# Fused attention and feed-forward layer: the first loads of v and of the weights wait for VectorE's first scores

## The chip, the cores and the metric

The kernel runs on one core of a Trainium2 chip. The metric is the device time of one execution in microseconds (us). Three runs of the kernel before took 865.44, 869.37 and 870.81 us; the median is 869.37 us.

The engines are called as in the profile: PE is TensorE (matmuls; PEld its weight loads), DVE is VectorE, ACT is ScalarE, POOL is GpSimd, SP is SyncE, which here only issues DMAs. SPq and ACTq are DMA issues on those two engines' queues.

## The reference

Sparse attention over 8 batches, 8 heads, 576 positions and a head size of 64, then a gated feed-forward layer over all 4608 tokens (512 to 2048 to 512), all in float32:

```python
scores = scale * np.matmul(q, k.transpose(0, 1, 3, 2))
mask_local = (rel >= 0) & (rel < stride)                    # stride = 32, heads 0 to 3
mask_strided = (rel >= 0) & (pos[None, :] % stride == pos[:, None] % stride)   # heads 4 to 7
scores = np.where(masks[None, :, :, :], scores, -1000000000.0)
attn = softmax(scores)          # exp of scores minus the row's maximum, divided by the sum plus 1e-9
x = np.matmul(attn, v)          # heads side by side: (4608, 512)
h = x @ w_in
g = h * np.clip(h + 3.0, 0.0, 6.0) / 6.0
out = g @ w_out
```

(`softmax` stands for three lines of the reference.)

## The kernel before, in words

**Attention.** A unit of work is a pair of heads of one batch (`pair`, L441). Batch 0 is pairs 0 to 3 in the order 0, 2, 1, 3 of their columns: in the names of tiles the digit is that column, so `qn_0`, `v_00` and `v_01` belong to the first pair (local heads), `v_2` to the second (strided heads), `v_10` and `v_11` to the third (local) and `v_3` to the fourth (strided). For the pairs of batch 0 the chain is this:

- q and k are loaded in rows (L492); PE turns them upright with an identity matrix into PSUM (`qp`, `kp`, L372), and DVE or ACT copies them to SBUF (L516, L514).
- PE forms the scores block by block (`ps`, L609 for local heads, L601 for strided ones). DVE adds the mask to the local ones (L634) and sets a corner of 32x32 (L636); ACT copies the strided ones (L627).
- Maximum and sum over rows are DVE's (L645, L659, L662), the subtraction and the scaling POOL's (L649, L666), exp is ACT's (L653).
- The first pairs of local heads are turned again by PE (`pe`, L372), copied by ACT (L723) and multiplied with windows of v (`pv`, L389); the strided ones are transposed by DVE (L685) and multiplied at L738. ACT and DVE write the result as a high and a low half (L427, L430): these are x.

v of a local pair of batch 0 is loaded by six DMAs (`load_half_windows`, L374): overlapping windows of 64 positions, each row of a head a piece of 64 floats, 256 bytes. A strided pair takes four DMAs (L567). Both are issued by SP in `load_v`.

**Feed-forward.** Three tiles of 512 tokens are computed directly (`ffn`, L821): `ph` is x times w_in (L859 to L861, three matmuls, since each float32 factor is a high and a low half), ACT and DVE form the gate (L779, L782), ACT and POOL split it (L793, L797), `acc` is its product with w_out (L836 to L838). The rest goes through a scheme of fast matrix products with fewer multiplications; the change does not touch it.

**Weights.** w_in and w_out are cut into 32 parts of 128 x 512 (`weight_part`, L261; k is the part's number, four parts of w_in, four of w_out and so on). A part is loaded by one DMA of 512 KB on SP (L274, `rawi` or `rawo`), and then made into two halves by ACT (L282, L286), DVE (L290) and POOL or ACT (L304, L306, L309).

**The order.** No engine's order is written by hand. Every step is given to a planner (`Plan`, L61) by `op(engine, us, fn, reads, writes, due, ...)`: an engine, an assumed duration, the keys that it reads and writes, a due time, and for loads `early`, the time before which it isn't issued, and `after`, the time that the transfer is assumed to take. `emit` (L91) plays this through: the engine that can start first takes the step that can start first, of equal ones the one with the earlier due time. From this come the order of instructions on each engine and the places at which PE gets filler matmuls (`idle`, L1564): wherever PE would be without work for 0.64 us or more in the first 100 us of the plan, a 128x384 matmul on the identity matrix is put in (L1573), which the profile shows as "PE idle". The order is fixed when the program is built; on the chip each instruction waits for what it depends on, and what stands behind it on its engine waits with it.

At the start, SP issues two loads of q and ACT two of k, SP two more of q and two of k, and then the first v, as soon as VectorE has cleared its edges.

Of the kernel before, what the change touches and what calls it, by code (L numbers as in the profile page):

```python
# [28 lines left out]
PAD = 32  # L29
# [31 lines left out]
class Plan:  # L61
# [12 lines left out]
    def op(self, engine, us, fn, reads=(), writes=(), due=0.0, room=0.0, mode="", after=0.0, take=None, give=None, early=0.0):  # L74
        n = len(self.ops)
        before = set()
        for k in reads:
            if k in self.wrote:
                before.add(self.wrote[k])
            self.used.setdefault(k, []).append(n)  # L80
        for k in writes:
            if k in self.wrote:
                before.add(self.wrote[k])
            before.update(self.used.pop(k, ()))
            self.wrote[k] = n
        before.discard(n)
        how = engine if isinstance(engine, dict) else {engine: us}
        self.ops.append((how, fn, before, due, room, mode, after, take, give, early))
        return n
# [85 lines left out]
def attention_ffn(ctx: ExitStack, tc, q, k, v, w_in, w_out, out):  # L175
    nc = tc.nc
# [21 lines left out]
    op = plan.op  # L198
    tiles = {}
# [61 lines left out]
    def weight_part(k, w, g, i):  # L261
        key = wkey(w, g, i)
        fc = FQ * g if w == "i" else FQ * g + i + 1
        due = T0 + fc * TILE / NFC - 5.0 + 0.01 * k
        fkey = ("x", 1, 1 - (k // 2 % 2 if k < 20 else 0), k % 2)
        name = f"{w}{g}{i}"

        def load():
            if w == "i":
                src = w_in[i * P:(i + 1) * P, g * TOK:(g + 1) * TOK]  # L270
            else:
                src = w_out[(g * FQ + i) * P:(g * FQ + i + 1) * P, :]
            raw = new(wp, key, [P, TOK, 2], I32, f"raw{name}")
            nc.sync.dma_start(raw, src.bitcast(I32).rearrange("p (n t) -> p n t", t=2))  # L274

        def bits():
            raw = tiles[key]
            return raw.rearrange("p n t -> p (n t)")[:, :TOK]

        def high():  # L280
            f = new(xp, fkey, [P, TOK], I32, f"f{name}")
            nc.scalar.activation(f.bitcast(F32), tiles[key][:, :, 1].bitcast(F32), AF.Prelu, scale=2.0 ** -112, alpha=2.0 ** 32)  # L282

        def low():
            raw = tiles[key].bitcast(U16).rearrange("p n (t u) -> p n t u", u=2)[:, :, 0, 1]
            nc.scalar.activation(bits(), raw, AF.Copy, scale=2.0 ** -13, bias=2.0 ** -14 - 0.5)  # L286

        def join():
            f = tiles[fkey]
            nc.vector.scalar_tensor_tensor(out=f, in0=f, scalar=3, in1=bits(),  # L290
                                           op0=ALU.logical_shift_left, op1=ALU.bitwise_or)

        def whole():
            f = tiles[fkey].bitcast(F32)
            return f if w == "i" else f.rearrange("p (h e d) -> p h d e", h=2, d=2)

        def part(x):
            t = tiles[key][:, x]
            return t if w == "i" else t.rearrange("p (h d e) -> p h d e", h=2, d=2)

        def hi(e):
            new(wp, key, [P, 2, TOK], F32R, f"w{name}")
            if e == "ACT":
                nc.scalar.copy(part(0), whole())  # L304
            else:
                nc.gpsimd.tensor_copy(part(0), whole())  # L306

        def lo():
            nc.gpsimd.tensor_tensor(out=part(1), in0=whole(), in1=part(0).bitcast(F32), op=ALU.subtract)  # L309

        op("SP", 0.53, load, writes=[key], due=-49 + 0.01 * k if k < 4 else -48.4 + 0.01 * k if k < 6 else -2 + 0.1 * k if k < 16 else due - 20.0, early=7.0 if k < 16 else due - 30.0, after=1.6 if k < 16 else 1.25)
        op("ACT", 0.68, high, reads=[key], writes=[fkey], due=due - 5, room=LATE + 1.0)
        op("ACT", 0.68, low, writes=[key], due=due - 5)
        op("DVE", 1.05, join, reads=[key], writes=[fkey], due=due - 3)
        op(HIENG, 0, hi, reads=[fkey], writes=[key], due=due - 2)
        op("POOL", 1.3, lo, reads=[fkey, key], writes=[key + ("lo",), key], due=due - 1)
# [124 lines left out]
    def pair(g):  # L441
# [3 lines left out]
        loc = h0 < H // 2  # L445
        nm = f"{b}_{c}"
        early = (b == 0) + (g == 0)
        due = timing(g)
# [90 lines left out]
        first = b == 0 and loc  # L539
# [18 lines left out]
        def load_v():  # L558
# [6 lines left out]
            rows = v[b, h0:h0 + 2].rearrange("j (m a t) d -> a m j (t d)", a=4, t=8)  # L565
            for a in range(4):
                nc.sync.dma_start(tiles[vkey][PAD * a:PAD * a + NPOS].rearrange("p j t d -> p j (t d)"), rows[a])  # L567
        op("SP", 2.6 if first else 1.6 if loc else 2.1, load_v, writes=vkeys, due=(-52, -48.8, -48.7, -48.5)[g] if early else due - 30, early=0 if early else due - 35, after=3.2 if first else 2.0)


        ekeys = [("el" if loc else "es", j) for j in range(2)]
# [42 lines left out]
        for j in range(2):  # L614
            sd = due - 12 + 4 * j
            ek, st = ekeys[j], stkey + (j,)
            pool = (0.9 if loc else 0.5) if b > 1 else 0.1 + 0.002 * cols
            red = 0.18 + 0.00095 * cols

            def keep(j=j):  # L620
                if j == 0:
                    new(ap, stkey, [P, 2, 2, 8], F32, f"st{nm}")
                if wide:
                    ps = tiles[banks[j].key][:, :2 * cols].rearrange("p (u z x) -> p u z x", z=2, x=w)
                    for a in range(4):
                        rows = slice(PAD * a, PAD * a + PAD)
                        nc.scalar.copy(e_of(j)[rows], ps[rows, :, a % 2])  # L627
                    return
                ps = tiles[banks[j].key][:n, :cols].rearrange("p (u x) -> p u x", x=w)
                m = (mband if loc else mtri)[:n].unsqueeze(1).to_broadcast([n, nblk, w])  # L630
                if soft:
                    nc.vector.scalar_tensor_tensor(out=e_of(j), in0=ps, scalar=SCALE, in1=m, op0=ALU.mult, op1=ALU.add)
                else:
                    nc.vector.tensor_tensor(out=e_of(j), in0=ps, in1=m, op=ALU.add)  # L634
                if loc:
                    nc.vector.memset(e_of(j)[:PAD, 0, :PAD], NEG)  # L636
            op("ACT" if wide else "DVE", 4 * 0.28 if wide else 0.17 + 0.00102 * cols + 0.08 * loc, keep, reads=[banks[j], "const"],
               writes=[ek, st], give=banks[j], due=sd + 0.5)
            if wide:
                def masked(j=j):  # L640
                    nc.gpsimd.tensor_tensor(out=e_of(j), in0=e_of(j), in1=mtri.unsqueeze(1).to_broadcast([n, nblk, w]), op=ALU.add)  # L641
                op("POOL", pool, masked, reads=["const"], writes=[ek], due=sd + 0.6)

            def most(j=j):
                nc.vector.tensor_reduce(out=st_of(j, 0), in_=e_of(j), axis=AX.X, op=ALU.max, negate=True if soft else None)  # L645

            def less(j=j):
                x = e_of(j)
                nc.gpsimd.tensor_tensor(out=x, in0=x, in1=st_of(j, 0).unsqueeze(2).to_broadcast(x.shape), op=ALU.subtract)  # L649

            def exp(j=j):
                if not soft:
                    nc.scalar.activation(e_of(j), e_of(j), AF.Exp, scale=SCALE)  # L653
                    return
                for u in range(nblk):
                    nc.scalar.activation(e_of(j)[:, u], e_of(j)[:, u], AF.Exp, bias=st_of(j, 0)[:, u:u + 1])

            def total(j=j):
                nc.vector.tensor_reduce(out=st_of(j, 1), in_=e_whole(j)[:, :, :w + 1], axis=AX.X, op=ALU.add)  # L659

            def inverse(j=j):
                nc.vector.reciprocal(st_of(j, 1), st_of(j, 1))  # L662

            def norm(j=j):
                x = e_of(j)
                nc.gpsimd.tensor_tensor(out=x, in0=x, in1=st_of(j, 1).unsqueeze(2).to_broadcast(x.shape), op=ALU.mult)  # L666
            op("DVE", red, most, reads=[ek], writes=[st], due=sd + 0.7)
            if not soft:
                op("POOL", pool, less, reads=[st], writes=[ek], due=sd + 1)
            op("ACT", 1.45 if soft else 0.2 + 0.00085 * cols, exp, reads=[st] if soft else [], writes=[ek], due=sd + 1.5)  # L670
            op("DVE", red, total, reads=[ek], writes=[st], due=sd + 2)
            op("DVE", 0.21, inverse, writes=[st], due=sd + 2.1)
            op("POOL", pool, norm, reads=[st], writes=[ek], due=sd + 2.5)
# [933 lines left out]
```

## Time and profile before

| | |
|---|---|
| median of 3 runs | 869.37 us (865.44 to 870.81) |
| the profiled execution, its own time | 871.91 us |
| its span, first to last instruction | 869.8 us |
| mean granted clock of PE | 0.986 of full speed |
| busy: PE, POOL, ACT, DVE | 850.1, 611.4, 562.6, 537.9 us |
| moved by DMA | 179.12 MB, mean 206 GB/s |

How to read it: busy time is the sum of an engine's instructions as the profiler recorded them. A row of "stretches" gives, for a piece of the span, the busy us of PE, PEld, DVE, ACT and POOL with the number of instructions in brackets, then PE's granted clock, the mean busy share of the 16 DMA engines and what they moved in GB/s. "under 512 B" in a row on DMA counts the packets smaller than that. A row of the chain of waits is the start in us, the length in us, and the engine and line that the end was waiting for at that time; "issue" is time in which the engine waited for nothing that the profile shows. A row of the timeline is start, length, engine, line, operation, names, and xN for N merged instructions. A product in full float32 counts as two matmuls: 12 calls in the program are x24 in the profile.

### The profile page before, as it was taken

Reading aid. Unit: us, or ns where it says so; the run is one execution under the profiler, and the core shown is the slowest. Engines: PE = TensorE matmul, PEld = TensorE weight load, DVE = VectorE, ACT = ScalarE, POOL = GpSimd, SP = SyncE. Lnnn points to the kernel's source line nnn. Section 1 sums busy time; section 2 is a strip of 40 time slices with the busy share of each in tenths; the row PEclk is TensorE's granted clock in tenths of the full one; section 3 lists DMA queues with packets and bytes.
Section 4 is the critical chain, followed back from the end, with each engine's and each line's share of the span. In section 5 each row is a group of like instructions: output and inputs, shape, how many; then the busy total and the mean of one; then the engine's idle time right before and its main releaser. Section 6 shows DMA issues by size and latency. Waiting matters only on the chain.

```text
span 869.8 us, 18939 instructions
## 1 busy us (share of the span) xinstructions
PE 850.1 (98%) x6954; PEld 686.3 (79%) x6954; DVE 537.9 (62%) x902; ACT 562.6 (65%) x1245; POOL 611.4 (70%) x603
## 2 busy tenths in 40 slices
PE   8999999999999999999999999999999999999996
PEld 6767787888888888888888888788888778888884
DVE  5588878434544538554556555566777888555586
ACT  3587657788778775977778865677654645454441
POOL 4588977588447899766677994455874987767573
PEclk9699999999999999999999999999999999999998
DMA  8968722789974445898999998778666667866536
GB/s 207 313 139 227 229 55 68 210 267 268 299 203 100 132 126 147 241 276 213 270 266 292 286 295 232 214 212 218 187 182 192 188 177 225 242 197 193 182 122 145
DMA packets 323308, 179.12 MB, mean 206 GB/s; under 512 B 182864, under 2 KB 300368, under 8 KB 323216
## 3 DMA queue, kind: packets, MB, share of 16 engines
q1 hardware_dynamic: 318564, 176.27, 71.8%
q10 hardware_dynamic: 4652, 1.64, 0.9%
q8 instruction: 55, 0.90, 0.4%
q14 instruction: 37, 0.30, 0.1%
HBM read 136.97 MB, written 40.89 MB: 205 GB/s over the span
## 4 chain that ended last, share of the span: by engine, by line
PE 87%; POOL 5%; DVE 4%; issue 1%; ACT 1%; DMA 1%; SPq 1%; POOLq 0%; ACTq 0%
PE P L1132 8%; PE P L1133 8%; PE P L1134 8%; PE cP L1455 5%; PE cP L1457 5%; PE cP L1456 5%; PE ph L859 5%; PE acc L836 5%; PE ph L861 4%; PE ph L860 4%; PE acc L838 4%; PE acc L837 4%; PE acc L1217 4%; PE acc L1219 3%; PE acc L1218 3%; PE pv L400 2%
## 5 line engine op out<-in xcount | busy, mean ns | idle before, releaser
L1473 DVE SCALAR_TENSOR_TENSOR C<-cP,C 128x512 f32<-128x512 f32 x96 | 65.7, 687 | 39.3 <-PE cP L1457 38.5
L797 POOL TENSOR_TENSOR gl<-u,gh 128x512 fp32r<-128x512 f32 x48 | 65.3, 1363 | 34.7 <-ACT gh L793 20.3
L1144 DVE TENSOR_TENSOR G<-P,G 128x512 f32<-128x512 f32 x64 | 44.0, 688 | 55.7 <-PE P L1134 43.2
L1132 PE MATMUL P<-B_T,wr 128*128 128x512 f32 x192 | 75.6, 394 | 2.3 <-DVE G L1144 1.6
L836 PE MATMUL acc<-wo,gh 128*128 128x512 f32 x192 | 76.8, 400 | 0.0
L838 PE MATMUL acc<-wo,gl 128*128 128x512 f32 x192 | 75.2, 392 | 0.2 <-POOL gl L797 0.2
L837 PE MATMUL acc<-wo,gh 128*128 128x512 f32 x192 | 74.9, 390 | 0.0
L1134 PE MATMUL P<-B_T,wr 128*128 128x512 f32 x192 | 74.8, 390 | 0.0
L1133 PE MATMUL P<-B_T,wr 128*128 128x512 f32 x192 | 74.8, 389 | 0.0
L1370 POOL TENSOR_TENSOR sp<-G,sp 128x512 fp32r<-128x512 f32 x34 | 47.2, 1399 | 24.1 <-ACT sp L1366 24.1
L1139 ACT COPY G<-P 128x512 f32<-128x512 f32 x64 | 37.6, 587 | 40.0 <-PE P L1134 39.6
L666 POOL TENSOR_TENSOR e<-e,st 96x384 f32<-96x384 f32 (+1 forms) x64 | 43.9, 689 | 25.1 <-DVE st L662 23.8
L859 PE MATMUL ph<-x,wi 128*128 128x512 f32 x128 | 52.6, 411 | 2.3 <-ACT x L427 1.2
L782 DVE SCALAR_TENSOR_TENSOR u<-u,ph 128x512 f32<-128x512 f32 x48 | 32.6, 682 | 34.0 <-ACT u L779 33.9
L701 ACT COPY atloc<-e 32x192 f32<-32x192 f32 x144 | 50.9, 353 | 3.8 <-DVE e L691 1.5
L659 DVE TENSOR_REDUCE st<-e 96x6 f32<-96x390 f32 (+1 forms) x64 | 27.2, 428 | 42.3 <-ACT e L653 21.3
L860 PE MATMUL ph<-x,wi 128*128 128x512 f32 x128 | 50.7, 396 | 0.6 <-DVE x L430 0.5
L861 PE MATMUL ph<-x,wi 128*128 128x512 f32 x128 | 50.8, 397 | 0.0
L1132 PE MATMUL P<-B_B,wr 128*128 128x512 f32 x120 | 47.6, 397 | 1.2 <-DMA wr<-dA 0.7
L779 ACT ACTIVATE u<-ph,three 128x512 f32<-128x512 f32 x48 | 33.0, 687 | 24.3 <-PE ph L861 23.8
L645 DVE TENSOR_REDUCE st<-e 96x6 f32<-96x384 f32 (+1 forms) x64 | 25.8, 414 | 36.1 <-POOL e L641 35.8
L1133 PE MATMUL P<-B_B,wr 128*128 128x512 f32 x120 | 46.8, 390 | 0.0
(604 smaller groups left out, 2683.5 us busy)
## 6 DMA issues: line engine op xcount, KB each, us to landing
wr<-dA SPq DMA_DIRECT2D x72, 256.0 KB
or<-do SPq DMA_DIRECT2D x32, 512.0 KB
wr<-dSu SPq DMA_DIRECT2D x48, 256.0 KB
wr<-dSv SPq DMA_DIRECT2D x48, 256.0 KB
or<-do SPq DMA_DIRECT2D x48, 256.0 KB
rawi<-in_moe_w_in_dram SPq DMA_DIRECT2D x16, 512.0 KB
rawo<-in_moe_w_out_dram SPq DMA_DIRECT2D x16, 512.0 KB
do<-wo SPq DMA_DIRECT2D x16, 512.0 KB
```

The lines of the kernel that those rows point to most:

```text
L701: nc.scalar.copy(at[PAD * (a + h):PAD * (a + h) + PAD, :, rows], e[rows, :, PAD * h:PAD * h + PAD])
L797: (nc.vector if tail else nc.gpsimd).tensor_tensor(out=to, in0=src(), in1=tiles[gk[0]].bitcast(F32), op=ALU.subtract)
L836: nc.tensor.matmul(acc, gh, woh, start=fc == 0, stop=False)
L837: nc.tensor.matmul(acc, gh, wol, start=False, stop=False)
L838: nc.tensor.matmul(acc, gl, woh, start=False, stop=end)
L859: nc.tensor.matmul(ph, wih, xh, start=n_ == 0, stop=False)
L860: nc.tensor.matmul(ph, wih, xl, start=False, stop=False)
L861: nc.tensor.matmul(ph, wil, xh, start=False, stop=n_ == NCC - 1)
L1132: nc.tensor.matmul(ph, wh, xh, start=fresh and k == 0, stop=False, skip_group_check=not fresh)
L1133: nc.tensor.matmul(ph, wh, xl, start=False, stop=False, skip_group_check=not fresh)
L1134: nc.tensor.matmul(ph, wl, xh, start=False, stop=k == 1, skip_group_check=not fresh)
L1473: nc.vector.scalar_tensor_tensor(out=tiles[ck], in0=tiles[bank], scalar=1.0 / 6.0, in1=tiles[ck], op0=ALU.mult, op1=ALU.add)
```

## The change

A key `gate` is added to the planner's bookkeeping. It is written by a new step on VectorE: a memset of one element of the first pair's v tile, in its edge of zeros, placed right after the first pair's first scores have been written to SBUF and depending on them. The loads of v of batch 0 and the loads of the first 16 parts of the weights (k below 16) read `gate`, so SP issues none of them before that memset. The load of the first pair's v is registered at that place instead of at its old one; the other pairs' loads stay where they were.

```diff
-        op("SP", 0.53, load, writes=[key], due=-49 + 0.01 * k if k < 4 else -48.4 + 0.01 * k if k < 6 else -2 + 0.1 * k if k < 16 else due - 20.0, early=7.0 if k < 16 else due - 30.0, after=1.6 if k < 16 else 1.25)
+        op("SP", 0.53, load, reads=["gate"] if k < 16 else [], writes=[key], due=-49 + 0.01 * k if k < 4 else -48.4 + 0.01 * k if k < 6 else -2 + 0.1 * k if k < 16 else due - 20.0, early=7.0 if k < 16 else due - 30.0, after=1.6 if k < 16 else 1.25)
...
-        op("SP", 2.6 if first else 1.6 if loc else 2.1, load_v, writes=vkeys, due=(-52, -48.8, -48.7, -48.5)[g] if early else due - 30, early=0 if early else due - 35, after=3.2 if first else 2.0)
+        def get_v():
+            op("SP", 2.6 if first else 1.6 if loc else 2.1, load_v, reads=["gate"] if early else [], writes=vkeys, due=(-52, -48.8, -48.7, -48.5)[g] if early else due - 30, early=0 if early else due - 35, after=3.2 if first else 2.0)
+        if g:
+            get_v()
...
             op("ACT" if wide else "DVE", 4 * 0.28 if wide else 0.17 + 0.00102 * cols + 0.08 * loc, keep, reads=[banks[j], "const"],
                writes=[ek, st], give=banks[j], due=sd + 0.5)
+            if g == 0 and j == 0:
+                op("DVE", 0.07, lambda: nc.vector.memset(tiles[vkeys[0]][PAD:PAD + 1, 0, :1], 0.0), reads=[ek], writes=[*vkeys, "gate"], due=sd + 0.5)
+                get_v()
```

Lines behind the edit move by 4, and from the middle of `pair` on by 7: L634 becomes L638, L738 becomes L745, L1573 becomes L1580.

On VectorE the new memset does not stand right behind the first sum (the planner lets the second head's sum go first). Before, from the first sum on:

```order
L634 TENSOR_TENSOR e_130<-ps_00_357,mband 96x6x64
L636 MEMSET e_130 32x32
L634 TENSOR_TENSOR e_228<-ps_01_358,mband 96x6x64
L636 MEMSET e_228 32x32
L645 TENSOR_REDUCE st_0_417<-e_130 96x6
L645 TENSOR_REDUCE st_0_417<-e_228 96x6
```

Now:

```order
L638 TENSOR_TENSOR e_130<-ps_00_339,mband 96x6x64
L640 MEMSET e_130 32x32
L638 TENSOR_TENSOR e_228<-ps_01_340,mband 96x6x64
L640 MEMSET e_228 32x32
L644 MEMSET v_00_237 1x1
L652 TENSOR_REDUCE st_0_393<-e_130 96x6
```

One row is added, the one at L644, the fifth after the first scores arrive; nothing else on VectorE moves there.

On SP, behind the six loads of q and k and the six of the first pair's v (the last of which is the first row here), before:

```order
L381 DMA v_01_239<-in_v_dram 64x9x64
L567 DMA v_2_241<-in_v_dram 18x2x512 x4
L274 DMA rawi_329<-in_moe_w_in_dram 128x1024
L274 DMA rawi_331<-in_moe_w_in_dram 128x1024
L274 DMA rawi_353<-in_moe_w_in_dram 128x1024
L274 DMA rawi_355<-in_moe_w_in_dram 128x1024
L378 DMA v_10_257<-in_v_dram 32x64
```

Now:

```order
L381 DMA v_01_239<-in_v_dram 64x9x64
L274 DMA rawi_487<-in_moe_w_in_dram 128x1024
L274 DMA rawi_493<-in_moe_w_in_dram 128x1024
L274 DMA rawi_497<-in_moe_w_in_dram 128x1024
L274 DMA rawi_522<-in_moe_w_in_dram 128x1024
L567 DMA v_2_241<-in_v_dram 18x2x512 x4
L378 DMA v_10_251<-in_v_dram 32x64
```

The order is the same but for the second pair's v, which now goes behind the first four parts of the weights. All of these rows, and the six before them, stand behind the wait for `gate`.

On PE the same work comes in nearly the same order. Between the first pair's second turn (`pe_00`, `pe_01`) and that of the third pair (`pe_10`) stood before:

```order
L372 MATMUL pe_00_551<-ident,e_130 64x96 x6
L372 MATMUL pe_01_578<-ident,e_228 64x96 x6
...
L389 MATMUL pv_01_635<-at_195,v_01_239 64x32
L1573 MATMUL idle<-ident 128x384 x3
L738 MATMUL pv_20_705<-atstr_266,v_2_241 64x72
...
L601 MATMUL ps_31_735<-kt_3_285,qt_3_284 64x36
L1573 MATMUL idle<-ident 128x384 x3
L372 MATMUL pe_10_797<-ident,e_130 64x96 x6
```

Now:

```order
L372 MATMUL pe_00_530<-ident,e_130 64x96 x6
L1580 MATMUL idle<-ident 128x384
L372 MATMUL pe_01_550<-ident,e_228 64x96 x6
...
L1580 MATMUL idle<-ident 128x384 x3
L605 MATMUL ps_30_686<-kt_3_279,qt_3_278 64x36
...
L745 MATMUL pv_21_729<-atstr_262,v_2_241 64x72
L1580 MATMUL idle<-ident 128x384
L372 MATMUL pe_10_775<-ident,e_130 64x96 x6
```

The second pair's products (`pv_2`) and the fourth pair's scores (`ps_3`) change places, and the fillers stand elsewhere: one in the first pair's turn, one instead of three ahead of `pe_10`, and three more behind it, ahead of the first `ph`. Further on, small differences in the planner's times exchange neighbouring steps on all engines for the rest of the program; the work is the same.

## The prediction

> **What bounds the kernel now.** I read the page first, then stretches of 5 us, then the chain of waits in order of time, then the DMA queues in narrow windows, and last the timeline of the engines that the change touches.
>
> From the page: the span, the busy time of the engines, and the clock that TensorE was granted in 40 slices.
>
> ```profile
> span 869.8 us, 18939 instructions
> PE 850.1 (98%) x6954; PEld 686.3 (79%) x6954; DVE 537.9 (62%) x902; ACT 562.6 (65%) x1245; POOL 611.4 (70%) x603
> PEclk9699999999999999999999999999999999999998
> ```
>
> TensorE (PE) is busy 98% of the span, so an edit to the opening can only bring what PE loses there. The second slice has 6 instead of 9: the clock is not full for a while. The stretches (engine busy us and instructions, granted clock, DMA share, GB/s) say when:
>
> ```profile
> 15.00:20.00 5.00, 3.37 (x108) 2.95 (x103) 1.85 (x5) 2.54 (x7) 2.13 (x4) 0.89 0.77 189
> 20.00:25.00 5.00, 5.00 (x52) 3.92 (x54) 2.31 (x8) 1.77 (x7) 2.12 (x6) 0.50 1.05 349
> 34.00:36.00 2.00, 2.00 (x24) 1.33 (x24) 0.00 (x0) 0.05 (x1) 1.92 (x3) 0.51 1.01 391
> 36.00:38.00 2.00, 2.00 (x82) 1.75 (x79) 1.40 (x3) 1.37 (x5) 0.55 (x1) 1.00 0.98 328
> 160.00:869.00 709.00, 697.66 (x5014) 567.22 (x5012) 422.74 (x666) 457.11 (x1026) 498.86 (x473) 1.00 0.75 212
> ```
>
> From just before 20 us to 36 us the clock is 0.50. After 160 us PE idles 11.34 of 709 us. The chain of waits (start, us, what) runs through PE almost without a break from 6 to 45 us:
>
> ```profile
> 8.32 1.00 PE qp L372 x32
> 10.71 0.76 issue
> 11.46 0.83 PE ps L609 x56
> 13.43 0.84 PE idle L1573 x2
> 14.27 1.14 PE kp L372 x24
> 15.41 0.41 PE ps L601 x17
> 15.82 1.63 issue
> 17.45 0.90 PE ps L601 x47
> 18.35 1.60 PE qp L372 x32
> 19.95 1.58 PE idle L1573 x2
> 21.53 2.12 PE kp L372 x32
> 23.65 2.29 PE pe L372 x24
> 28.82 0.73 issue
> 29.54 1.06 PE pv L389 x19
> 30.61 4.14 PE idle L1573 x6
> 34.74 1.75 PE pv L738 x32
> 37.56 2.13 PE idle L1573 x6
> 40.55 0.43 PE ph L859
> 44.58 1.19 PE pv L389 x72
> 51.30 2.27 DMA vstr<-in_v_dram
> 115.90 1.15 PE pv L738 x32
> ```
>
> ("PE idle" are filler matmuls that the plan puts in, not idleness; the last row is a later one, for comparison.) Three pieces are "issue", time in which PE waited for nothing that the profile shows: 0.76, 1.63 and 0.73 us, each in the middle of a run of equal matmuls. The queue of instruction loads explains them. First the whole span's row, then counts of PE between the ends of the three pieces, then the queue's row in 14.0 to 14.5 us:
>
> ```profile
> q8 instruction: 55, 0.90, 0.4%
> 11.46:15.82 4.36, 4.36 (x127) 3.37 (x126) 2.75 (x7) 1.56 (x3) 1.53 (x2) 1.00 1.01 176
> 17.45:29.00 11.55, 11.37 (x253) 9.57 (x254) 6.21 (x19) 6.14 (x17) 4.24 (x9) 0.56 0.88 251
> q8 instruction: 1, 0.02, 17.5%
> ```
>
> 55 packets go with 6954 matmuls and as many weight loads: 253 instructions each, or 126 matmuls. The waits lie 127 and 2 x 126.5 matmuls apart, so each falls where a new block of PE's program begins. The block missing at 15.82 was loaded by the packet that began in 14.0 to 14.5 us and took 17.5% of 16 x 0.5 us = 1.4 us. My reading: a block is asked for when the one before it is begun (11.46), waits behind data (begins at 14.0 to 14.5) and is usable 11.46 to 17.45 = 6.0 us after the request. The clock falls 1.5 us after that wait.
>
> [...]
>
> **The change part by part.** The data that occupies the DMA engines at that time is v: in 256-byte pieces, 2 x (32 + 512 + 576) = 2240 for the first pair, by the shapes in the program. The rows of packets for 5 to 13 and 13 to 18 us, and then SP's issues and the instructions that count here:
>
> ```profile
> DMA packets 1659, 1.76 MB, mean 220 GB/s; under 512 B 798, under 2 KB 1174, under 8 KB 1658
> DMA packets 1817, 0.77 MB, mean 155 GB/s; under 512 B 1653, under 2 KB 1653, under 8 KB 1816
> 5.54 0.33 SPq L378 DMA_DIRECT2D v<-in_v_dram  x1
> 16.49 2.57 SPq L274 DMA_DIRECT2D rawi<-in_moe_w_in_dram  x4
> 13.68 0.09 DVE L636 MEMSET e<- 32x32 f32 x1
> 26.28 0.68 ACT L282 ACTIVATE fi<-rawi 128x512 f32<-128x512 f32 x1
> 27.32 1.49 PE L389 MATMUL pv<-at,v 64*64 64x32 f32 x44
> ```
>
> 1. Added: one memset of one element on VectorE (DVE). Next row up, the 32x32 memset: 0.09 us, so at most that, and DVE has slack there (1.85 us of 5 busy in 15 to 20). 0.
>
> 2. Moved: SP's issues from 5.54 to the end of DVE's fourth instruction on scores, 13.68 + 0.09 = 13.77, or about 13.5 with term 3. Everything behind on SP's queue waits too: six issues of the first v, weights, the other v. The two loads that matter next: the first pair's v is used at 27.32. Before, its pieces had landed by about 17.5 (798 + 1653 small packets by 18 us cover the 2240), 12 us after the first issue; with the same 12 us it lands at 25.5, with less competition earlier. The first weights are issued at 16.49 and used at 26.28. In the new order they come right behind the six v issues; at 0.33 to 0.64 us each (the row at 5.54, and 2.57 / 4) these end between 15.5 and 17.4, about the same time as now. So 0 for both, with 1 to 2 us of cover for v if PE gets there 3 us sooner; the cost if the cover goes is in the last rival. The strided v of the second pair goes behind the weights in spite of the title; its product comes after the three fillers of 4.14 us at 30.61, so 0.
>
> 3. Removed, the wait at 10.71 (0.76). Most of its delay is q and k, loaded as before; v joins only from 5.54. Between 0 and -0.76; I take -0.3, near the end where q and k dominate.
>
> 4. Removed, the wait at 15.82 (1.63). The block is asked for at 11.46 or sooner, when only the rest of q and k is in flight and v is held until 13.5. Between 0 and -1.63; I take all of it.
>
> 5. The next two blocks. They now meet the held loads. Without the wait PE crosses into the next block at 15.82 - 0.3 = 15.5; 126 matmuls on, in the middle of pe, is reached at about 15.5 + 0.90 (ps) + 1.00 (qp at full clock, row at 8.32) + 0.84 (filler) + 1.14 x 32/24 = 1.5 (kp) + 0.9 (half of pe at full clock) = 20.6 if nothing else waits, and its instructions are usable 4.6 to 6.0 us after 15.5, at 20.1 to 21.5. (4.6 is the fetch for 28.82: asked for at 24.9, by 126 matmuls from 17.45, usable at 29.54.) The block after that, asked for at about 21, is usable at 25.6 to 27; I take 26.3. Before, that point was 29.54. So PE stands 3.2 us earlier there, terms 3 and 4 (1.9) included, and 1.3 of it is from the clock; it waits about 2 us for instructions there, since at full clock it would arrive at about 24. Bounds: 0 (all is lost again) and, with no wait at all, 24 - 29.54 = -5.5.
>
> 6. The clock after 29.54. Excess at half clock in the rows: fillers 4.14 - 2.13 = 2.01, pv 1.06 - 1.19 x 19/72 = 0.75, pv of the second pair 1.75 - 1.15 = 0.60. Up to 3.3 us. As the 1.63 us wait was followed by half clock, the 2 us wait that I expect will be too, for part of it. I take -1.0 (0 to -3.3).
>
> [...]
>
> 7. Added: the new plan has ten filler rows for eight between 12 and 40 us (0.84 us each, row at 13.43, at full clock). They stand where PE would wait anyway, so between 0 and 1.7; I take 0.5.
>
> 8. All other instructions are re-planned, since the planner's clock moved. From 60 us PE is full, and what is gained by the first ph carries to the end as long as ACT, DVE and POOL start their weight splits earlier by as much; they wait for PE there. I take the carry as whole. The new order's own waits can differ by a few us either way, against the 11.34 us of idle PE above.
>
> Sum: -3.2 - 1.0 + 0.5 = **-3.7 us**. The profiled execution took 871.91 us, 2.1 over its span, and would take 868.2; it lies 2.5 above the median of the runs, 869.37, which gives **865.7 us**. Terms 5 and 6 at their ends give -5.5 - 3.3 = -8.8, and +1.7.
>
> **The rivals.**
>
> *The clock never falls.* If no block waits, terms 5 and 6 reach their ends: 869.4 - 8.8 = 860.6, and up to 1.5 better with all three issue waits and the slow rows before 29.54 counted from their starts. For it: with v held, the fetch for the 15.82 block is free. Against: the two fetches after it meet v and four loads of 512 KB at once.
>
> *The wait only moves.* The block after 15.5 or the one after that waits as much, the clock falls one block later, the fillers cost the rest: 869.4, or 868 to 871. For it: the fetch needed 4.6 to 6.0 us under any mix of loads so far, and the held loads are the same bytes in a shorter time. That the loads were no cause at all ends here too.
>
> *SP's queue stays late.* The gate opens 8.0 us after 5.54. If SP works off its list no faster than before, everything on it is 8.0 us late: the chain has vstr, a load, at 51.30 with 2.27 us, ahead of the work that starts the first tile, and the loads of the next q and k stand by it on the same queue. There the end moves by up to +8.0: 877.4. It decides from the point where SP is later at vstr than PE is earlier (3.7 us). Against: ten issues of v took SP from 5.54 to 16.49, 1.1 us each against 0.33 and 0.64 in its rows, so it was mostly waiting there while q and k were in flight, which the change ends; and the loads between (v, raw weights) are used many us after landing.
>
> **How the numbers follow.** Forecast 0.50, clock 0.15, moved 0.20, late queue 0.15. About 1%, 8.7 us, is what a measurement of this kernel can tell from no change: under 860.7 lie most of the clock case and a thin tail of the forecast, 0.12; over 878 some of the late queue, 0.07; the rest, 0.81, is within. The range goes from 858, below the clock case, to 874, half way into the late queue, and leaves out less than 2 in 10. The forecast's own range is 862 to 869.
>
> **What would show it.** Right: no issue piece near 15.5; an instruction packet in 11 to 13 us; clock still 1.00 at 20 us; an issue piece of 1 to 3 us in the first pv at 24 to 26; first ph at 36 to 38 instead of 40.55. Wrong: an issue piece over 1 us before 17 us or a clock that falls by 20; a first pv or an ACT conversion of raw weights that waits for DMA; a first ph later than 40.

## The result, and the profile after

The changed kernel took **875.46 us** (median of 10 runs, 872.92 to 876.52), the kernel before, on the same chip, 870.11 (10 runs, 865.44 to 872.08). The ratio is 1.0062, 95% interval 1.0044 to 1.0080: slower by 3.8 to 7.0 us, where 3.7 us less were forecast and the range ended at 874. The profiled execution took 872.92 us, the lowest of the ten, while the one of before (871.91) lies near the top of that kernel's range. Setting the two traces side by side therefore shows some 4 us less loss than there is; whatever is read from single traces below is good to about that, and the medians decide. All comparisons use fast executions; left out are one of before at 935.60 us and one of new_order_short_join at 3690.66.

The page of the changed kernel: the span, the busy times, the granted clock in 40 slices.

```profile
span 871.1 us, 18940 instructions
PE 847.9 (97%) x6958; PEld 682.9 (78%) x6958; DVE 548.5 (63%) x901; ACT 558.8 (64%) x1242; POOL 612.0 (70%) x608
PEclk9999999999999999999999999999999999999999
```

The 6 in the second slice is gone. PE is busy 2.2 us less than before and the span is longer all the same. VectorE (DVE) is busy 10.6 us *more* (537.9 before) with one instruction fewer: something on VectorE got longer. The chain of waits at the opening (start, us, what):

```profile
15.20 1.07 PE ps L605 x64
16.27 1.15 PE qp L372 x32
...
22.73 0.81 PE pv L389 x42
23.54 2.18 issue
25.72 0.61 PE pv L389 x23
```

The scores at 15.20 run through, where before 1.63 us of "issue" cut them at 15.82. The one wait left lies in the first `pv`, 2.18 us at 23.54. The queue of instruction loads in 11 to 12 us and in 23 to 24 us:

```profile
q8 instruction: 1, 0.02, 6.3%
```
```profile
q8 instruction: 1, 0.02, 6.0%
```

The first packet took 6.3% of 16 us, 1.0 us; it now runs at 11 to 12 us, no longer behind v, whose first load SP issues at 13.60. So the opening went as meant, and better. Where the gain went, the first and the last product with the weights of w_in in the first two tiles say (`ph`, one of its three lines; us of the first and the last start), in before and in the changed kernel:

```profile
L859 PE MATMUL ph<-x,wi x128: 387/389/628, 40.5 to 251.5; 128*128 128x512 f32 x128
```
```profile
L866 PE MATMUL ph<-x,wi x128: 387/389/692, 34.4 to 251.2; 128*128 128x512 f32 x128
```

PE starts this work 6.1 us earlier and ends it 0.3 us earlier. Nearly all the gain is spent between 40 and 160 us. The windows of that stretch (engine busy us and instructions, clock, DMA share, GB/s), before and after:

```profile
40.00:160.00 120.00, 116.89 (x1202) 91.81 (x1200) 90.78 (x172) 87.67 (x176) 94.83 (x90) 0.99 0.60 157
```
```profile
40.00:160.00 120.00, 112.04 (x1092) 87.31 (x1091) 95.63 (x168) 80.11 (x157) 86.01 (x82) 0.97 0.63 169
```

PE idles 8.0 us of 120 where it idled 3.1. What PE waited for in 30 to 160 us (total us, times, longest), before and after:

```profile
PE ph L859 <- DVE u L782: 1.1, 2, 0.8
PE ph L860 <- DVE x L430: 0.5, 1, 0.5
PE acc L838 <- POOL gl L797: 0.2, 1, 0.2
```
```profile
PE ph L866 <- DVE u L789: 2.8, 2, 2.0
PE ph L867 <- DVE x L430: 1.8, 2, 1.3
PE acc L845 <- POOL gl L804: 1.6, 2, 1.0
```

VectorE and GpSimd (POOL) are what is late. VectorE's costliest groups in 20 to 100 us name the instruction. It is the join of a raw weight's two halves, L290 in both kernels (`fi` for w_in, `fo` for w_out; instructions, busy us, mean ns, idle before). Before, then after:

```profile
L290 DVE SCALAR_TENSOR_TENSOR fi<-fi,rawi 128x512 int32<-128x512 int32 x12 | 11.4, 958 | 0.2 <-ACT rawi L286 0.2
L290 DVE SCALAR_TENSOR_TENSOR fo<-fo,rawo 128x512 int32<-128x512 int32 x10 | 8.4, 856 | 0.6 <-ACT rawo L286 0.6
```
```profile
L290 DVE SCALAR_TENSOR_TENSOR fi<-fi,rawi 128x512 int32<-128x512 int32 x12 | 17.3, 1452 | 2.3 <-ACT rawi L286 1.1 <-DMA vstr<-in_v_dram 1.0 <-POOL e L656 0.3
L290 DVE SCALAR_TENSOR_TENSOR fo<-fo,rawo 128x512 int32<-128x512 int32 x10 | 13.2, 1339 | 0.1
```

The same 22 joins take 30.5 us for 19.8. These 10.7 us are about all of the 10.6 us that VectorE is busier. The longest of them in the chain of waits and in the timeline, and GpSimd at the same time (start, us):

```profile
36.48 3.72 DVE fi L290
```
```profile
36.48 3.71 DVE L290 SCALAR_TENSOR_TENSOR fi<-fi,rawi 128x512 int32<-128x512 int32 x1
```
```profile
36.17 0.60 POOL L306 CAST wi<-fi 128x512 fp32r<-128x512 f32 x1
36.74 1.27 POOL L309 TENSOR_TENSOR wi<-fi,wi 128x512 fp32r<-128x512 f32 x1
37.98 0.42 POOL L656 TENSOR_TENSOR e<-e,st 128x144 f32<-128x144 f32 x1
38.37 1.27 POOL L309 TENSOR_TENSOR wi<-fi,wi 128x512 fp32r<-128x512 f32 x1
39.59 0.19 POOL L1547 MEMSET vloc<- 32x128 f32 x1
```

The join starts in the middle of a cast of GpSimd's (36.17), lasts as long as GpSimd goes from one instruction to the next without a gap, and ends at 40.19, once GpSimd has stopped (39.78; its next starts at 40.73). It is on the chain of waits, so its length is paid for; the longest join on before's chain between 20 and 160 us is 2.53 us. GpSimd's own subtractions keep their 1.27 us. Theory A: the re-planned order puts joins and GpSimd's subtractions (L309) side by side more often, and that costs more than the hold brings. Theory B, the late-queue rival of the prediction: the held loads come too late.

### The profile page after: what moved, and what is told of

Read it like the earlier page. It is cut to its first block, busy times and chain, and to the rows that moved or that the text cites. A ratio compares the mean times of both kernels' runs of the same rounds, so it can differ in the third digit from the quotient of the medians.

```text
span 871.1 us, 18940 instructions
## 1 busy us (share of the span) xinstructions
PE 847.9 (97%) x6958; PEld 682.9 (78%) x6958; DVE 548.5 (63%) x901; ACT 558.8 (64%) x1242; POOL 612.0 (70%) x608
## 4 chain that ended last, share of the span: by engine, by line
PE 87%; POOL 5%; DVE 4%; ACT 2%; issue 2%; DMA 1%; SPq 0%; POOLq 0%; ACTq 0%
PE P L1139 8%; PE P L1140 8%; PE P L1141 8%; PE acc L843 5%; PE cP L1462 5%; PE acc L845 5%; PE cP L1463 5%; PE cP L1464 5%; PE acc L844 5%; PE ph L866 5%; PE ph L867 4%; PE ph L868 4%; PE acc L1224 3%; PE acc L1225 3%; PE acc L1226 3%; PE pv L400 2%
## 5 line engine op out<-in xcount | busy, mean ns | idle before, releaser
L1146 ACT COPY G<-P 128x512 f32<-128x512 f32 x64 | 37.5, 586 | 46.0 <-PE P L1141 45.5
L673 POOL TENSOR_TENSOR e<-e,st 128x144 f32<-128x144 f32 (+1 forms) x64 | 42.7, 668 | 25.0 <-DVE st L669 23.5
L666 DVE TENSOR_REDUCE st<-e 128x8 f32<-128x152 f32 (+1 forms) x64 | 27.1, 426 | 35.6 <-ACT e L663 18.1
L1139 PE MATMUL P<-B_B,wr 128*128 128x512 f32 x120 | 47.3, 394 | 0.0
L1140 PE MATMUL P<-B_B,wr 128*128 128x512 f32 x120 | 46.8, 390 | 0.0
L1141 PE MATMUL P<-B_B,wr 128*128 128x512 f32 x120 | 46.7, 389 | 0.0
L1139 PEld LDWEIGHTS P<-B_T,wr 128*128 128x128 f32 x192 | 36.0, 188 | 13.2 <-ACT G L1146 3.3
```

Of the source, the lines that this page charges most:

```text
L1139: nc.tensor.matmul(ph, wh, xh, start=fresh and k == 0, stop=False, skip_group_check=not fresh)
L1140: nc.tensor.matmul(ph, wh, xl, start=False, stop=False, skip_group_check=not fresh)
L1141: nc.tensor.matmul(ph, wl, xh, start=False, stop=k == 1, skip_group_check=not fresh)
```

## The experiments

Runs of one group ran on one chip and share the runs of the kernel before. The interval of a difference of two ratios is put together here as the root of the sum of the squares of their half widths.

### Hold and order apart

**hold_old_order.** Before's order on every engine. The hold is made where the instructions are written out: SP's loads from the first v on come behind the memset.

```diff
+            if n == self.held_from:
+                held = [n]
+                continue
+            if held and e == "SP":
+                held.append(n)
+                continue
...
+            if n == self.opener:
+                self.gate()
+                for m in held:
+                    ops[m][1]()
+                held = None
```

> The hold alone: the instructions of every engine in the order of the kernel before, with VectorE's memset added and SP's loads from the first v on behind it. Theory A (the new plan's order loses what the hold gains: the weight joins on VectorE meet GpSimd's work more often): the waits at 10.71 and 15.82 us are gone, the first ph is 4 to 6 us earlier than in the kernel before, the joins average 0.9 to 1.0 us as before, and the time is 3 to 6 us under the kernel before, ratio 0.993 to 0.997. Theory B (the loads come too late, and that costs it): 3 to 6 us over the kernel before, ratio 1.004 to 1.007, with waits for DMA on ScalarE or TensorE.

**new_order_no_hold.** The changed kernel's order on every engine, with the memset writing into a constant, so that no load waits for it.

```diff
-                op("DVE", 0.07, lambda: nc.vector.memset(tiles[vkeys[0]][PAD:PAD + 1, 0, :1], 0.0), reads=[ek], ...
+                op("DVE", 0.07, lambda: nc.vector.memset(three[:1], 3.0), reads=[ek], ...
```

> The new plan's order on every engine, but the memset writes another tile, so that no load waits for it on the chip: v and the weights are issued as early as before. Theory A: the instruction wait at 15.8 us and the half clock are back and the new order's loss stays: 5 to 10 us over the kernel before, ratio 1.006 to 1.012, joins on VectorE at 1.2 us or more on the mean. Theory B: the loss is gone, ratio 0.998 to 1.002.

**changed_again.** The changed kernel once more, beside these.

> The changed kernel once more, beside the other two on this chip: ratio 1.004 to 1.008 by both theories. Its profile shows whether the head of 34.4 us to the first ph and the long joins come back.

| | median us | ratio to before | interval |
|---|---|---|---|
| before | 868.89 | 1 | |
| hold_old_order | 867.32 | 0.9983 | 0.9967 to 0.9999 |
| new_order_no_hold | 877.84 | 1.0087 | 1.0056 to 1.0119 |
| changed_again | 873.67 | 1.0063 | 1.0040 to 1.0085 |

With the hold in both, the new order costs 1.0063 - 0.9983 = 0.0080 ± 0.0028, that is 7.0 ± 2.4 us. Without a hold in either it costs 0.0087. The hold alone gains 1.5 us (0.1 to 2.9), less than the 3 to 6 expected, and in the new order 2.1 ± 3.4. Theory B falls: the order loses as much when no load is held. The windows of 40 to 160 us, of hold_old_order and of new_order_no_hold, agree (first number behind the 120.00: PE busy):

```profile
40.00:160.00 120.00, 116.77 (x1187) 91.59 (x1185) 89.46 (x172) 87.23 (x175) 93.38 (x86) 0.99 0.66 172
```
```profile
40.00:160.00 120.00, 111.29 (x1148) 86.58 (x1147) 97.68 (x167) 76.03 (x148) 88.12 (x85) 0.96 0.58 151
```

PE idles 3.2 us in the old order with the hold (3.1 without it, in before) and 8.7 in the new order without it (8.0 with it). The joins go with that: 981 and 858 ns on the mean in hold_old_order, 1597 and 1294 in new_order_no_hold (groups in 20 to 100 us). changed_again has 1472 and 1336 ns again; its first `ph` starts at 35.4 us, not 34.4.

One part of the expectation for new_order_no_hold missed. The waits for instructions came back, but not the half clock: PE's clock stayed at 1.00 up to 50 us in that profile. The waits were 1.92 us at 15.19, 1.66 at 22.38 and 0.91 at 27.10; the window of 20 to 25 us (the clock is third from the end):

```profile
20.00:25.00 5.00, 3.34 (x56) 2.52 (x57) 3.39 (x11) 2.17 (x8) 2.39 (x5) 1.00 0.91 252
```

Why the hold alone brings so little is in the chain of hold_old_order: the wait of 1.63 us at 15.82 is gone, and a longer one stands further on, in the first `pv`:

```profile
24.90 2.23 issue
```

Its first `ph` starts at 36.70, 3.8 us earlier than before's 40.5 (4 to 6 were expected), and its span is 2.3 us shorter.

### Joins beside GpSimd, by themselves

**joins_beside_gpsimd.** No work of the layer, only VectorE's instructions on 128x512, alone and beside a row of GpSimd's subtractions.

> None of the layer's work: only VectorE's join (two operands in SBUF, 128x512, int32) eight times while GpSimd is idle, eight times while GpSimd subtracts 128x512 tiles without a break, then eight multiplications with one SBUF operand and eight subtractions with one operand in PSUM, each beside GpSimd. Theory A: alone 0.65 to 0.70 us each; beside GpSimd over 1.3 us on the mean, single ones far longer; one SBUF operand and a PSUM operand as fast as alone. Rival (the joins are long for another reason, such as their semaphores): all within 10% of alone.

The groups (the first is GpSimd beside the joins and then beside TENSOR_SCALAR, the second GpSimd with VectorE idle; `beside` and `alone` are the joins):

```profile
L85 POOL TENSOR_TENSOR pa<-pa,fa 128x512 f32<-128x512 f32 x14 | 20.4, 1456 | 1.1
L85 POOL TENSOR_TENSOR pc<-pc,fa 128x512 f32<-128x512 f32 x14 | 17.7, 1262 | 1.1
L80 DVE SCALAR_TENSOR_TENSOR beside<-fa,bits 128x512 int32<-128x512 int32 x8 | 12.1, 1515 | 0.2
L96 DVE TENSOR_SCALAR single<-fa 128x512 f32<-128x512 f32 x7 | 9.6, 1366 | 0.2
L80 DVE SCALAR_TENSOR_TENSOR alone<-fa,bits 128x512 int32<-128x512 int32 x8 | 5.5, 690 | 0.2
L101 DVE TENSOR_TENSOR fromps<-ps,fa 128x512 f32<-128x512 f32 x7 | 4.8, 691 | 0.2
```

A join takes 690 ns alone and 1515 beside GpSimd; an instruction with one operand in PSUM took 691 beside GpSimd. That part of Theory A holds by itself. The expectation missed in one place: TENSOR_SCALAR, with one operand in SBUF, took 1366 ns beside GpSimd (neither of the two was timed alone).

One join in the layer lost more than one instruction's worth: that of 36.48 above took 3.0 us more than the 0.69 of a join alone, and no single instruction of GpSimd beside it took more than 1.27. Why the two take longer side by side is not shown by these runs.

### Is it the held loads, or any new plan?

**memset_in_plan_only.** The kernel before, with one more instruction of 0.07 us in the plan and nothing held.

```diff
+            if g == 0 and j == 0:
+                op("DVE", 0.07, lambda: nc.vector.memset(three[:1], 3.0), reads=[ek], writes=["gate"], due=sd + 0.5)
```

> The kernel before with the memset as one more instruction in the plan (0.07 us, on VectorE, into a constant), and nothing held: no load waits for it. The plan moves all the same: of VectorE's 856 rows 695 keep their order, of GpSimd's 583 rows 426. Theory A1 (the plan is sensitive: any re-planned order of the first 160 us is a new draw, and the one of before is a good draw): several us slower than before, 872 to 878, with more idle of TensorE in 40 to 160 us than the 3.1 us of before. Theory A2 (the order got worse because the planner was told that the held loads come late): within 1 us of before, 868 to 871.

**memset_costed_0_30.** The changed kernel with another cost of the memset in the plan.

```diff
-                op("DVE", 0.07, lambda: nc.vector.memset(tiles[vkeys[0]][PAD:PAD + 1, 0, :1], 0.0), ...
+                op("DVE", 0.30, lambda: nc.vector.memset(tiles[vkeys[0]][PAD:PAD + 1, 0, :1], 0.0), ...
```

> The changed kernel, hold included, with the planner's cost of the memset at 0.30 us for 0.07; the work is the same, the order is another (of VectorE's rows 718 of 859 stay in order). Theory A1: another draw, which may lie anywhere from 866 to 878 and by over 2 us from the changed kernel's 875. Theory A2: the hold is as late as before in the plan or 0.23 us later, so 874 to 877. TensorE's idle time in 40 to 160 us goes with the result in both.

Before took 869.86 here. memset_in_plan_only took **882.04** us (ratio 1.0149, 1.0125 to 1.0173): one instruction of 0.07 us, with no load waiting for it, costs 12 us by the order that it brings about. This is Theory A1, beyond its own range, and not Theory A2, which gave 868 to 871. PE's waits grew at two places. The first is the known stretch, where PE idles 6.6 us (row below). The second is 360 to 560 us, where PE idles 5.3 us for 0.5 before; there its chain has loads and a long VectorE instruction, none of them near the opening. That instruction (493.82, two operands in SBUF) took 4.58 us, where two of the same line at 715.45 took 2.30 together; but PE's longest wait there, 3.6 us for another VectorE instruction (L1146), was over before it began, so the joins and this instruction don't explain all of the 12 us:

```profile
40.00:160.00 120.00, 113.36 (x1171) 88.60 (x1170) 94.47 (x169) 80.58 (x159) 92.00 (x88) 0.99 0.59 156
...
360.00:560.00 200.00, 194.66 (x1618) 156.50 (x1616) 100.13 (x167) 136.98 (x325) 136.98 (x145) 0.99 0.88 248
```
```profile
437.27 6.50 DMA or<-do
443.83 5.77 DMA or<-do
...
481.20 6.48 DMA or<-do
...
493.82 4.58 DVE G L784
```

memset_costed_0_30 took 875.53 (1.0068, 1.0048 to 1.0089), the same as the changed kernel. That is what Theory A2 gave; Theory A1 allowed it, but had looked for a time over 2 us away. By itself it decides nothing.

### Does the contention carry the cost?

Contention here means only that joins take longer beside GpSimd's work, 1515 ns for 690. Two pairs, each with the old and the new order and the hold in both. In the first GpSimd's subtraction gives way to a memset, which reads nothing; in the second VectorE's join becomes short while GpSimd's work stays. Both leave out part of the work and are read for their time alone. Both also take work off an engine: a memset takes 0.52 us where a subtraction takes 1.3 to 1.4, and short joins save VectorE 13.6 us in 20 to 100 us (16.9 for 30.5 in the new order; 25 or more had been expected).

**old_order_no_subtract** and **new_order_no_subtract**:

```diff
         def lo():
+            if k < 16:
+                nc.gpsimd.memset(part(1).bitcast(F32), 0.0)
+                return
             nc.gpsimd.tensor_tensor(out=part(1), in0=whole(), in1=part(0).bitcast(F32), op=ALU.subtract)
```

> Before's order with the hold, and GpSimd's subtraction that makes the low half of a weight replaced by a memset of zeros for the first 16 weight tiles (that half of these weights is left out of the result). To be read against the next run alone. Theory A (VectorE's joins meet GpSimd's subtractions and take up to twice as long): the joins fall from about 0.92 us to 0.7 to 0.8, and since joins were hardly in the way in this order, the time falls by 0 to 2 us from 867.3. Rival (what counts is the position of the joins, not their length): the same.

> The changed kernel with the same replacement. Theory A: the joins fall from about 1.40 us to 0.7 to 0.8, VectorE gets some 10 us back in 20 to 100 us, TensorE's idle time in 40 to 160 us falls from 8 to about 3, and the time comes within 1.5 us of the run with the old order (gap now 7 us). Rival: the gap stays at 4 us or more though the joins are short.

**old_order_short_join** and **new_order_short_join**:

```diff
+            few = slice(None) if k >= 16 else slice(8)
-            nc.vector.scalar_tensor_tensor(out=f, in0=f, scalar=3, in1=bits(),
+            nc.vector.scalar_tensor_tensor(out=f[:, few], in0=f[:, few], scalar=3, in1=bits()[:, few],
```

> Before's order with the hold, and VectorE's join for the first 16 weight tiles done on 8 columns for 512 (so the upper and the lower bits of these weights are joined in 8 columns only). GpSimd's subtractions stay at full size. To be read against the next run. If the joins' length on VectorE carries the cost of the new order: 865 to 867, since VectorE is hardly in the way in this order. If GpSimd's own time carries it: 866 to 868.

> The changed kernel with the same short joins. If the joins' length on VectorE carries the cost of the new order: VectorE gets 25 us or more back in 20 to 100 us, TensorE's idle time in 40 to 160 us falls from 8 to about 3, and the time is within 1.5 us of the run with the old order. If it is GpSimd's time (subtractions that the joins stretch, so that gl and the low halves come late) or the position of the work: the gap stays at 3 us or more.

| hold in all | old order, us (ratio) | new order, us (ratio) | new less old |
|---|---|---|---|
| all work | 867.32 (0.9983) | 873.67 (1.0063) | 7.0 ± 2.4 us |
| no subtraction | 865.17 (0.9948) | 865.77 (0.9959) | 1.0 ± 2.0 us |
| short joins | 865.82 (0.9952) | 868.70 (0.9978) | 2.3 ± 1.9 us |

The last column is the difference of the ratios times 870. Without the subtractions the gap between the orders is closed within the interval, and PE idles alike in both. The joins (new order) and the windows of 40 to 160 us (old, then new):

```profile
L290 DVE SCALAR_TENSOR_TENSOR fi<-fi,rawi 128x512 int32<-128x512 int32 x12 | 10.2, 862 | 2.4 <-ACT rawi L286 2.4
L290 DVE SCALAR_TENSOR_TENSOR fo<-fo,rawo 128x512 int32<-128x512 int32 x10 | 8.1, 826 | 0.1
```
```profile
40.00:160.00 120.00, 116.44 (x1149) 91.98 (x1149) 89.37 (x172) 87.84 (x179) 83.48 (x90) 1.00 0.69 175
```
```profile
40.00:160.00 120.00, 116.71 (x1209) 92.69 (x1209) 89.53 (x172) 86.06 (x173) 81.24 (x90) 1.00 0.70 183
```

The joins fall from 1452 and 1339 to 862 and 826 ns, VectorE gets 12.2 of 30.5 us back, and PE idles 3.3 us in the new order for 8.0 (3.6 in the old). The joins did not fall to the 0.7 to 0.8 us expected. Short joins alone, with GpSimd's subtractions as they were, close 4.7 ± 3.1 of the 7 us (PE idles 3.8 us in the new order, 5.1 in the old), so time on VectorE is a part of it, by the middle value the larger one. The remaining 2.3 lies between the 1.5 that this theory allowed and the 3 of its rivals, and the interval holds both. The first `ph` does not settle it: new_order_short_join's starts at 36.37 and old_order_short_join's at 33.78, but the first pair differs by as much (37.5 and 34.5) and its times agree. The rival "position, not length" predicted gaps of 4 and 3 us and falls in the first pair; in the second its lower bound lies inside the interval.

What the two pairs don't separate is the contention from the work that they take off an engine. For the contention speaks that the two orders hold the same instructions and differ in the length of the joins, and that over the eight profiles with all the work PE's idle time in 40 to 160 us rises roughly with the mean of the joins in 20 to 100 us: 3.1 and 3.2 us idle at 0.90 and 0.91 us (before, hold_old_order), 6.6 and 5.1 at 1.16 and 1.21 (memset_in_plan_only, joins_costed_1_4 below), 7.8 to 8.7 at 1.39 to 1.46 (the changed kernel, changed_again, memset_costed_0_30, new_order_no_hold).

### Telling the planner

**joins_costed_1_4.** The changed kernel, joins planned at 1.4 us:

```diff
-        op("DVE", 1.05, join, reads=[key], writes=[fkey], due=due - 3)
+        op("DVE", 1.4 if k < 16 else 1.05, join, reads=[key], writes=[fkey], due=due - 3)
```

> The changed kernel with the planner's cost of the first 16 weight tiles' joins raised from 1.05 to 1.4 us, about what they took in its profile; the work is the same. If the new order is bad because the planner puts its work on VectorE by too low a cost: better than the changed kernel by 3 us or more, 867 to 872. If each re-plan is a draw that the costs do not steer: anywhere from 866 to 882, with joins of another length and idle time of TensorE in 40 to 160 us that goes with the result.

It took 873.28 us (869.91 to 878.46; ratio 1.0051, 1.0032 to 1.0070), about the changed kernel's, so a truer cost is no cure: the 3 us that one theory expected did not come. All four re-planned orders (the changed kernel's, and those of memset_in_plan_only, memset_costed_0_30 and this run) are slower than before's, by 3.7 to 12.2 us; no new plan here was better. Its joins became 1153 and 1308 ns, and PE idles 5.1 us in 40 to 160. What a join takes depends on what GpSimd does at that moment (690 ns with GpSimd idle, 1515 beside its subtractions in joins_beside_gpsimd), which one number per instruction can't hold. Of the kernels that do all the work, hold_old_order is the fastest, with an interval that just excludes before.

## Why the prediction was wrong, step by step

1. *The memset costs nothing.* On the chip, yes: it took 0.06 us, at 13.52. In the plan it does not: memset_in_plan_only shows 12 us for one like it. This was not seen.

2. *Both late loads are covered.* Nearly. The first `pv` did not wait for v (a later product waited 0.2 us). The first four raw weights were issued from 18.45 us on, for 16.49 before, and a conversion of ScalarE's (L282) waited 0.8 us for one (1.4 in hold_old_order, none in before). A wait of 1.0 us of VectorE for `vstr` is in the group of joins above; SP issues it at 54.23 us for 51.30. These waits don't explain the loss: new_order_no_hold holds no load and is no faster.

3 and 4. *The waits at 10.71 and 15.82 go.* Both are gone from the chain, the first wholly (0.3 of its 0.76 was taken).

5. *The point that was 29.54 stands at 26.3, after about 2 us of waiting in the first `pv`.* It was 25.72, after 2.18 us. The reading of the fetches held in this: the packet came late (23 to 24 us), and the point came where the reading put it. Counted back from 25.72 by 126 matmuls each, blocks begin at about 20.9, 15.6 and 11.4 us in this trace, and the packets begin at 23.3, 16.0 and 11.9: two about half a us after a block, the third 2.4 us after one, with the held loads in flight.

6. *Half clock again after that wait; -1.0.* In the profiled execution the clock stayed full. From that point to the first `ph` it took 8.7 us where before took 11.0: 2.3 less, of the 3.3 that the term counted at most. In changed_again, after a wait of 2.19 us, the clock was not full. The windows of 25 to 30 us, of the changed kernel's profile and of changed_again (the clock is third from the end):

```profile
25.00:30.00 5.00, 4.08 (x107) 2.88 (x108) 4.59 (x12) 3.08 (x8) 1.92 (x4) 1.00 0.76 220
```
```profile
25.00:30.00 5.00, 4.56 (x60) 2.57 (x61) 4.59 (x13) 2.73 (x6) 1.98 (x3) 0.69 0.80 195
```

After a wait of about 2 us (2.18 and 2.19) the clock was full in one of these two executions and not in the other. So first `ph` started at 34.4 us where 36 to 38 was predicted (35.4 in changed_again).

7. *Two more filler rows, +0.5.* The fillers took as long as before, more of them at full clock: 22 instructions and 12.4 us before, 26 and 12.3 us now, up to 40 us.

8. *"I take the carry as whole. The new order's own waits can differ by a few us either way."* **This is the step that failed.** It named the danger and then put no term into the sum for it. The order cost 7.0 ± 2.4 us with the hold, and by the two pairs above most or all of it goes away when the joins or GpSimd's subtractions are made light: the longer joins say that in the new order the two meet more often. A look at the joins in the trace of before would have warned: their groups took 856 and 958 ns on the mean, single ones from 0.65 to 2.52 us, so their length was not a property of the instruction. It could not have given the sign or the size.

With the new order at 7.0 and the hold at the 1.5 us that it gains in the old order, the sum is +5.5. That is changed_again taken apart, and no separate check; the first group's +5.4 (3.8 to 7.0) agrees with it. What the hold brings was mis-sized too: 3.7 us forecast, 1.5 (0.1 to 2.9) measured with the order held, though the first `ph` came 3.8 us earlier in that profile. So even with the old order the carry was not seen to be whole.

*The rivals.* That the clock never falls was true of the profiled execution up to 50 us, and the time was not 860.6 because of step 8. "The wait only moves" describes hold_old_order: the wait at 15.82 went and 2.23 us at 24.90 came. "SP's queue stays late" gave 877.4, near the measured time, by a mechanism that the runs refute: with nothing held the new order is no faster (877.84 against 873.67 us). The rival that was missing is a re-planned order whose joins take longer beside GpSimd's work.

*What stays open.* The changed kernel's runs spread from 872.9 to 876.5 us over the two groups, and both profiles lie at the low end, so where the slower of them lose more was not seen. The part of the 7 us that is contention, and not simply more work on VectorE or GpSimd than the place allows, is not measured by itself, and what makes memset_in_plan_only lose its second 5 us is not shown. Nor was it tried whether the joins can be kept from meeting the subtractions without another plan.

## What to carry to other kernels

Where a planner sets the order, an edit has two effects, what it does on the chip and the order that it brings about. The second can be the larger one (here 7 us against 1.5, and 12 us for an instruction that no load waits for), so build the edit once with the old order and measure the two apart. Before an early gain is carried to the end, look for instructions whose mean differs from place to place in the trace: their length may depend on a neighbour, and a new order can change it (here the joins: 690 ns alone, 1515 beside GpSimd's subtractions). Comparing the two orders alone showed only that the order costs; making the suspected neighbours light in both orders showed where. Making one neighbour light also takes work off its engine, so do it for each of the two in turn.

## What the runs showed of the hardware that was not expected

- One join (VectorE, two operands in SBUF) lost more than one GpSimd instruction's time: 3.71 us at 36.48 for 0.69 alone, over the rest of a cast and four more instructions of GpSimd in a row (to 39.78). In the run by itself about one join went through per subtraction: 1515 ns for 690, and GpSimd's subtraction took 1456 on the mean beside the joins and TENSOR_SCALAR, for 1262 alone.
- The clock fell after a wait of 1.63 us in before and of 2.19 us in changed_again, and stayed at 1.00 after 2.18 us in the profiled execution of the changed kernel and after 1.92 and 1.66 us in that of new_order_no_hold.
